# Seven products for the first group's third unit, and later stores of the direct quarters

## The chip, the cores and the metric

The kernel runs on one core of a Trainium2 chip. The core has five engines that run side by side and meet at semaphores: TensorE (PE, matrix products; its weight loads are listed as PEld), VectorE (DVE), ScalarE (ACT), GpSimd (POOL) and SyncE (SP). In this kernel GpSimd and SyncE mainly issue transfers between the chip's DRAM and the on-chip memory (SBUF), and products land in the eight banks of PSUM. Each engine executes its instructions strictly in its own order: an instruction that waits holds up everything behind it on that engine. The metric is the time on the device of one execution, in microseconds (us).

## The reference

Two stages follow each other. A causal linear attention with decay runs over q, k, v of shape (4 batches, 8 heads, 768 positions, 64), in blocks with a running state per head:

```python
intra = einsum(einsum(qb, kb) * Dmask, vb)            # within the block
inter = einsum(qb * lam_pow, kv_state)                # from the blocks before
out[:, :, sl] = intra + inter
kv_state = lam_block * kv_state + einsum(kb * rev_pow, vb)
```

Its output, seen as x of 3072 tokens x 512, goes through a two-layer block in fp32, with w_in of 512 x 2048 and w_out of 2048 x 512:

```python
h = x @ w_in
g = h - tanh(h)
out = g @ w_out
```

## The kernel before, in words

**Groups and units.** The tokens are worked in six groups (g = 0 to 5) of 512: 128 positions of each of the four batches. The hidden dimension 2048 is worked in four units (u = 0 to 3) of 512. One unit of `h` is a 512 x 512 product; its four corners, 11, 12, 21 and 22, are 256 x 256 each, and a corner sits in one PSUM bank.

**Seven products in the place of eight.** From group 1 on, a unit is made by `up` (L545): seven block products with sums of quarters as factors (a Strassen-Winograd scheme), each four matmuls of 128x128 weights by 256 columns, so 28 in the place of the 32 that the plain form takes. The sums of weight quarters are made by `sums_in(u)` (L256, four VectorE additions, the last of which overwrite a quarter of the weights), those of token quarters by `att_sums(g)` (L509, four more). A product's result is not a corner: product 1's bank `y` is copied by ScalarE into a second bank `w` (L568), on which product 2 then accumulates; products 6 and 7 go on in `y`, products 5 and 3 in `z`, and VectorE adds the parts together. From group 2 on, some of these products are themselves made of seven smaller ones ("twice": `inner_steps`, L674, and `down_twice`, L895).

**Group 0** uses the plain form for all four units (`up_plain`, L954), since the weights arrive while it runs. They come as 64-bit words (the float64 input) that must be rounded to fp32: three ScalarE operations (L291 to L293) and two VectorE operations (L295, L296) for each block of 128 x 512 (`round_block`, called through `weights`). The list `turns` (L1062) writes out in which order units 1 to 3 are computed, how many blocks are rounded after each, and which piece of the next group's attention (`p0`, `p1`) is put behind it. Then `down_first` (L985) makes group 0's second layer in eight steps kt, with seven accumulating banks; `sums_out(kt)` makes the sums of w_out's quarters, and `sums_late`, `sums_first` those of the hidden values.

**Factors in DRAM.** `sums_out` stores the seven factors of w_out to a DRAM tensor `factors`. For products that are made twice, each factor is again needed as seven quarters and sums of quarters; these lie in the DRAM tensor `fine`, one slot of 256 KB for each. Of the seven, three are plain quarters of one factor ("direct"), and four are sums. Before, the direct ones are written in `sums_out` (L276 to L279), straight from the tiles there: 24 DMA issues over the eight steps, in rows of 512 bytes. The sums are made later in `factors_twice(t)` (L772), for t = 0 to 4, from four quarters that `load_quarters(t)` (L759) has read back from `factors`: t = 0 and 1 in group 1, t = 2 at the end of group 1, t = 3 and 4 in group 2. For t = 2 to 4 the four sums are written over the loaded quarters, in the tile `gS` (the hidden tensor "S1", free just then).

**The queue of loads.** During the groups, GpSimd issues every load of a weight piece (`piece`, L785) into a ring of eight tiles `wb`: it issues a load once the product that used the ring's oldest tile is done. Its other DMAs (stores of results, of `fine`, loads of quarters) stand in the same order, and each of its DMAs also waits for the eighth one before it.

**Who sets the order.** A tile framework orders each engine's instructions by priority and dependency, save those marked with `tied` or `keep_in_program_order`, which stay in program order on their engine. It adds every semaphore wait, those for a transfer that still reads a buffer about to be overwritten among them.

Of the kernel before, what the change touches and what calls it, by code (L numbers as in the profile page):

```python
# [16 lines left out]
AL = mybir.AluOpType  # L17
# [7 lines left out]
def kernel(  # L25
# [223 lines left out]
    def pair_tiles(kt):  # L249

        if kt % 3 == 2:
            return tuple(ws[u].rearrange("p x k c -> p (x k) c")[:, 0:4] for u in (3, 2))
        wt = wst.tile([128, 8, 256], F32, name="wt", tag="w")
        return wt[:, 0:4], wt[:, 4:8]

# [7 lines left out]
    def sums_out(kt):  # L263
        bt, tt = pair[kt]
        b11, b12, b21, b22 = (bt[:, x] for x in range(4))
        t1, t2, t4, t3 = (tt[:, x] for x in range(4))
        nc.vector.tensor_tensor(t1, b12, b11, op=AL.subtract)
        nc.vector.tensor_tensor(t2, b22, t1, op=AL.subtract)
        nc.vector.tensor_tensor(t3, b22, b12, op=AL.subtract)
        nc.vector.tensor_tensor(t4, b21, t2, op=AL.subtract)  # L270
        f = factors[:].rearrange("x p k c -> p x k c")
        nc.gpsimd.dma_start(out=f[:, 0:1, kt, :], in_=bt[:, 0:1, :])
        nc.gpsimd.dma_start(out=f[:, 1:3, kt, :], in_=bt[:, 2:4, :])
        nc.gpsimd.dma_start(out=f[:, 3:NX, kt, :], in_=tt[:, 0:4, :])

        for x, j in ((1, 0),) if kt % 2 == 0 else ((2, 0), (3, 1)):  # L276
            dst = fine[:, SUB.index(x), :, kt // 2, :].rearrange("n p c -> p n c")
            nc.gpsimd.dma_start(out=dst[:, 0:1], in_=bt[:, 3:4, ts(j, 128)])
            nc.gpsimd.dma_start(out=dst[:, 1:5], in_=tt[:, 0:4, ts(j, 128)])  # L279

    def round_block(w, raw64, first):

# [129 lines left out]
    def att_state(g, bs):  # L412
        pair_ = slice(bs[0], bs[0] + 2)
        if g == 0:
            kv = bank("kv", "att", 4).rearrange("d (b p e) -> d b p e", b=2, p=NP)
            for n, b in enumerate(bs):
                kd, vn = raw[g, b]["k"], raw[g, b]["v"]
                for p in range(NP):
                    for j in range(2):
                        tc.keep_in_program_order(nc.tensor.matmul(  # L420
                            out=kv[ts(j, 64), n, p, :], lhsT=kd[:, 2 * p + j, :], rhs=vn[:, 2 * p + j, :],
                            start=n == 0 and p == 0, stop=True, skip_group_check=True))
            tc.keep_in_program_order(nc.scalar.activation(states(1)[0][:, pair_], kv, AF.Copy))
            return


        old, mid, new = (x[:, pair_] for x in states(g))
        subs = (0, 1) if g < NG - 1 else (0,)
        kv = [bank("kv", "att", 4).rearrange("d (b p e) -> d b p e", b=2, p=NP) for _ in subs]
        for p in range(NP):  # L430
            nc.scalar.activation(mid[:, :, p], old[:, :, p], AF.Copy, scale=fwd[:, p, HALF - 1:HALF])
# [77 lines left out]
    def att_sums(g, bs):  # L509
        x0, x1 = xt[g, 0], xt[g, 1]  # L510
        b11, b21, b12, b22 = x0[:, 0:2], x0[:, 2:4], x1[:, 0:2], x1[:, 2:4]
        tt = xpool.tile([128, 3, 2, HB], F32, name="tt", tag="tt")
        nc.vector.tensor_tensor(tt[:, 0], b12, b11, op=AL.subtract)
        nc.vector.tensor_tensor(tt[:, 1], b22, tt[:, 0], op=AL.subtract)
        nc.vector.tensor_tensor(b12, b22, b12, op=AL.subtract)
        nc.vector.tensor_tensor(tt[:, 2], b21, tt[:, 1], op=AL.subtract)
        xt[g] = dict(B11=b11, B21=b21, B22=b22, T1=tt[:, 0], T2=tt[:, 1], T3=b12, T4=tt[:, 2])
# [27 lines left out]
    def up(g, u, n):  # L545
# [5 lines left out]
        t, first = product_bank(key, n)  # L551
        for m in range(2):
            for kt in range(2):
                nc.tensor.matmul(out=t[:, m, :], lhsT=wt[:, kt, ts(m, 128)], rhs=x[:, kt, :],  # L554
                                 start=first and m == 0 and kt == 0, stop=kt == 1, skip_group_check=True)

        def dst(c):
            return hidden(g, c)[:, u]
# [200 lines left out]
    def load_quarters(t):  # L759

        for i in range(2):
            for j in range(2):
# [6 lines left out]
                tied(t > 1, nc.gpsimd.dma_start(out=x, in_=quarter_source(t, i, j)))  # L769
                quarters[t, i, j] = x  # L770

    def factors_twice(t):  # L772

        b11, b12, b21, b22 = (quarters.pop((t, i, j)) for i in range(2) for j in range(2))
        if t > 1:
            t1, t3, t4, t2 = b11, b12, b21, b22
        else:
            t1, t2, t3, t4 = (late["pool"].tile([128, NU, 128], F32, name=f"wt{x}", tag="sums", bufs=4)
                              for x in (1, 2, 3, 4))
        for x, dst, a, b in ((5, t1, b12, b11), (7, t3, b22, b12), (6, t2, b22, t1), (4, t4, b21, t2)):  # L780
            tc.keep_in_program_order(nc.vector.tensor_tensor(dst, a, b, op=AL.subtract))
            nc.gpsimd.dma_start(out=fine[TWICE.index(MADE[t]), SUB.index(x)], in_=dst)
            yield
# [152 lines left out]
    def every(steps):  # L936
        for _ in steps:
            pass
# [15 lines left out]
    def up_plain(u, cs):  # L954

        hm = {}
        for c in cs:
            a, t = divmod(c - 11, 10)
            tag = ("att", 4) if u == 1 else (("ya", "yb", "z", "w")[2 * t + a], 1)
            hm[c] = bank("h", *tag).rearrange("q (m c) -> q m c", m=2)  # L960
        for i in range(KI):
            for c in cs:
                a, t = divmod(c - 11, 10)
# [15 lines left out]

    def sums_first(u):  # L980
        g11, g12, g22, s1 = (hidden(0, c)[:, u] for c in (11, 12, 22, "S1"))
        nc.vector.tensor_tensor(s1, g12, g22, op=AL.add)
        nc.vector.tensor_tensor(g12, g11, g12, op=AL.subtract)

    def down_first(kt, ns):  # L985

# [65 lines left out]
    for i in range(KI - 1):  # L1052
        next(rest)
        next(rest)
        if i:
# [3 lines left out]
    every(rest)  # L1059
    sums_first(0)  # L1060
    p0, p1 = attention(1)
    turns = [(1, 11, 2, ()), (1, 21, 2, ()), (1, 12, 2, ()), (1, 22, 2, ()), (2, 11, 0, ()), (2, 21, 1, p0[0:1]),  # L1062
             (3, 11, 0, p0[1:3]), (3, 21, 1, p0[3:4]), (2, 12, 1, p0[4:]), (2, 22, 1, p1[0:1]), (3, 12, 1, p1[1:3]),
             (3, 22, 1, ())]
    for u, c, n, more in turns:
        every(up_plain(u, (c,)))
        ahead = (u, c) == (2, 12)
        if ahead:
            run(more)
        weights(ready["done"] + n, u > 1)  # L1070
        if not ahead:
            run(more)
        if c == 22:
            sums_first(u)
            if u == 1:
                ready["to"] = len(blocks)
                load(B + 2)
                load_weights(NU * KI + 2)
                load(B + 3)
                load_weights(NU * KI + WAHEAD)  # L1080
                load(2 * B)
                powers()
    sums_out(0)
    weights(NU * KI + 6, True)
    for kt in range(KH):
        down_first(kt, (1, 2))
        if kt == 0:
            run(p1[3:4])
            down_first(kt, (5,))
            run(p1[4:])  # L1090
        if kt + 1 < KH:
            sums_out(kt + 1)
        sums_late(kt)
        down_first(kt, (4, 7, 6, 3) if kt == 0 else (5, 4, 7, 6, 3) if kt + 1 < KH else (5, 6, 7, 4, 3))
        if kt + 3 < KH:
            weights(ready["done"] + 2)
        if kt in (1, 4, 6):
            sums_in((1, 4, 6).index(kt))
    first_results()
    early.close()  # L1100
    late["blk"] = ctx.enter_context(tc.tile_pool(name="blk", bufs=2 * B - 1))
# [6 lines left out]
    def make_factors(step):  # L1108
        t = TURNS.get(step)
        if t is not None:  # L1110
            if t not in making:
                making[t] = factors_twice(t)
            next(making[t])

# [4 lines left out]
    for g in range(1, NG):  # L1119
# [84 lines left out]
        if last:  # L1204
            down_end(g)
            continue
        if g < GI:
            for u in (2, 3):
                inner_weights(u, (6,))
# [5 lines left out]
        for kind, x in in_turn(g):  # L1215
# [19 lines left out]
                every(factors_twice(3))  # L1235
            if g == GI and (kind, x) == (5, 6):
                load_quarters(4)
            if g == GI and (kind, x) == (6, 7):
                every(factors_twice(4))
            if kind == 6 and x in (5, 6, 2, 7):  # L1240
# [35 lines left out]
```

## Time and profile before

| | us |
|---|---|
| runs (median of 3) | 649.3 (646.28 to 653.39) |
| the profiled execution | 649.38 |
| its span, first to last instruction | 647.6 |
| TensorE busy | 635.9 |
| VectorE / ScalarE / GpSimd busy | 477.6 / 267.3 / 228.6 |

The span is 1.8 us below the profiled execution's own time. TensorE's granted clock is full throughout. Busy times of TensorE are of pipelined instructions whose ends are modelled. "Idle before" in a row is how long the engine stood still ahead of that instruction, with what released it. A time such as 351.48 is counted from the span's start.

### The profile page before, as it was taken

How to read it: one execution, taken by the hardware profiler on the slowest of the kernel's cores; microseconds unless marked ns; L12 is line 12 of the kernel's file. 1: busy time of each engine (PE TensorE's matmuls, PEld its weight loads, DVE VectorE, ACT ScalarE, POOL GpSimd, SP SyncE). 2: the span in 40 equal slices, each digit the busy share in tenths (PEclk: the TensorE clock that was granted, in tenths of full speed). 3: DMA queues.
4: the chain of work that ended last, by engine and by line, in shares of the span. 5: the costliest groups of instructions: out<-in, count | busy, mean ns of one | idle time of the engine just before them, and what ended most of it. 6: DMA issues, size and time to landing. Idle time of an engine off the chain costs nothing.

```text
span 647.6 us, 16635 instructions
## 1 busy us (share of the span) xinstructions
PE 635.9 (98%) x6440; PEld 584.0 (90%) x6440; DVE 477.6 (74%) x948; ACT 267.3 (41%) x620; POOL 228.6 (35%) x397
## 2 busy tenths in 40 slices
PE   8899999999999999999999999999999999999998
PEld 7788888888888899998999998999998899998997
DVE  4468697785898867569967569988667987467953
ACT  4789676503432422345331247333245332334310
POOL 0000255735443454410455431355321254520161
PEclk9999999999999999999999999999999999999999
DMA  9979998969765999775889986798884577832484
GB/s 215 219 192 245 315 273 278 346 191 266 207 167 124 294 264 303 210 191 121 211 242 289 289 211 160 173 280 242 261 182 96 134 237 241 246 104 76 102 287 150
DMA packets 166190, 139.80 MB, mean 216 GB/s; under 512 B 136864, under 2 KB 138016, under 8 KB 166112
## 3 DMA queue, kind: packets, MB, share of 16 engines
q0 software_dynamic: 31792, 104.62, 51.1%
q1 hardware_dynamic: 134176, 34.12, 26.2%
q8 instruction: 51, 0.84, 0.6%
q14 instruction: 27, 0.22, 0.1%
q10 hardware_dynamic: 144, 0.00, 0.0%
HBM read 111.94 MB, written 26.74 MB: 214 GB/s over the span
## 4 chain that ended last, share of the span: by engine, by line
PE 46%; issue 19%; DMA 10%; DVE 8%; POOL 8%; SPq 6%; ACT 3%; POOLq 0%; DVEq 0%; ACTq 0%
PE acc L994 7%; PE h L965 6%; DMA q_blk<-in_q_dram 5%; PE y L906 5%; SPq L151 4%; PE plain L849 4%; PE y L554 4%; POOL wb L795 4%; PE zw L906 3%; PE y L697 3%; PE z L554 2%; POOL wb L792 2%; DMA k_blk<-in_k_dram 2%; DMA k_nat<-in_k_dram 1%; PE z L697 1%
## 5 line engine op out<-in xcount | busy, mean ns | idle before, releaser
L795 POOL DMA_DIRECT2D wb<-fine x133 | 71.7, 540 | 159.2 <-PE plain L849 108.8
L849 PE MATMUL plain<-wb,g 128*128 128x256 f32 x416 | 96.0, 381 | 0.0
L849 PEld LDWEIGHTS plain<-wb,g 128*128 128x128 f32 x416 | 77.5, 190 | 10.4
L965 PE MATMUL h<-xt,w 128*128 128x256 f32 x256 | 58.3, 382 | 1.4 <-DVE w L296 1.4
L798 POOL DMA_DIRECT2D wb<-factors x64 | 34.5, 540 | 71.2 <-PE z L697 47.9
L910 ACT ACTIVATE q<-y 128x128 f32<-128x128 f32 x76 | 21.1, 278 | 87.4 <-PE y L906 86.3
L965 PEld LDWEIGHTS h<-xt,w 128*128 128x128 f32 x256 | 47.5, 190 | 8.7 <-DVE w L296 1.8
L906 PE MATMUL y<-wb,g 128*128 128x128 f32 x336 | 44.8, 278 | 0.0
L792 POOL DMA_DIRECT2D wb<-fine_in x60 | 32.5, 544 | 28.8 <-PE z L697 10.8
L600 ACT ACTIVATE th<-g 128x512 f32<-128x512 f32 x48 | 29.4, 627 | 29.8 <-DVE g L625 29.6
L906 PEld LDWEIGHTS y<-wb,g 128*128 128x128 f32 x336 | 40.7, 192 | 0.7
L688 ACT ACTIVATE g<-y 128x512 f32<-128x512 f32 x24 | 14.3, 597 | 63.1 <-PE y L697 63.1
L404 ACT ACTIVATE k_nat<-k_nat,mask 128x64 f32<-128x64 f32 (+1 forms) x128 | 35.0, 335 | 1.7 <-DMA k_nat<-in_k_dram 1.7
L994 PE MATMUL acc<-wt,g 128*128 128x256 f32 x144 | 32.9, 380 | 0.2 <-DVE g L973 0.2
L601 DVE TENSOR_TENSOR g<-g,th 128x512 f32<-128x512 f32 x48 | 32.1, 683 | 0.4
L697 PE MATMUL z<-tt,wb 128*128 128x128 f32 x256 | 31.9, 275 | 0.0
L994 PEld LDWEIGHTS acc<-wt,g 128*128 128x128 f32 x144 | 27.2, 190 | 4.3 <-DVE g L973 0.6
L906 PE MATMUL zw<-wb,g 128*128 128x128 f32 x224 | 30.2, 278 | 0.1
L619 PE MATMUL y<-xt,w 128*128 128x256 f32 x128 | 30.3, 379 | 0.0
L619 PE MATMUL zs<-xt,ws 128*128 128x256 f32 x128 | 30.2, 379 | 0.0
L697 PEld LDWEIGHTS z<-tt,wb 128*128 128x128 f32 x256 | 30.2, 192 | 0.0
L292 ACT ACTIVATE r<-raw 128x512 int16<-128x512 uint32 x32 | 25.2, 787 | 8.8 <-DMA raw<-in_moe_w_out_dram 4.6
(236 smaller groups left out, 1475.0 us busy)
## 6 DMA issues: line engine op xcount, KB each, us to landing
wb<-fine POOLq DMA_DIRECT2D x133, 256.0 KB, 4.0
wb<-factors POOLq DMA_DIRECT2D x64, 256.0 KB, 4.3
wb<-fine_in POOLq DMA_DIRECT2D x60, 256.0 KB, 4.8
v_nat<-in_v_dram SPq DMA_DIRECT2D x24, 256.0 KB, 5.2
raw<-in_moe_w_out_dram POOLq DMA_DIRECT2D x12, 512.0 KB, 6.0
k_nat<-in_k_dram SPq DMA_DIRECT2D x20, 256.0 KB, 4.9
fine<-wt POOLq DMA_DIRECT2D x17, 256.0 KB, 3.5
raw<-in_moe_w_in_dram SPq DMA_DIRECT2D x8, 512.0 KB, 5.0
```

The source lines that it names most:

```text
L404: tc.keep_in_program_order(nc.scalar.activation(k_h, k_h, AF.Copy, scale=mask[0:rows, h % 2, h // 2, HALF - 1:HALF]))
L554: nc.tensor.matmul(out=t[:, m, :], lhsT=wt[:, kt, ts(m, 128)], rhs=x[:, kt, :], start=first and m == 0 and kt == 0, stop=kt == 1, skip_gro ...
L601: nc.vector.tensor_tensor(dst(c), src, th, op=AL.subtract)
L619: nc.tensor.matmul(out=t[:, m, :], lhsT=wt[:, kt, ts(m, 128)], rhs=x[:, kt, :], start=False, stop=kt == 1, skip_group_check=True)
L697: nc.tensor.matmul(out=dst[:, ts(u, 128)], lhsT=a, rhs=b, start=(x in (1, 5) or x == 2 and not filled) and u == 0, stop=True, skip_group_c ...
L792: nc.gpsimd.dma_start(out=t.rearrange("p m c -> p (m c)"), in_=fine_in[INNER.index(n_[1]), (5, 6, 3).index(x_)].rearrange("p u c -> p (u c)"))
L795: nc.gpsimd.dma_start(out=t.rearrange("p m c -> p (m c)"), in_=fine[TWICE.index(n_), SUB.index(x_)].rearrange("p u c -> p (u c)"))
L798: nc.gpsimd.dma_start(out=t, in_=factors[XAT[FACT[n_][1]]][:, 2 * x_:2 * x_ + 2, :])
L849: tied(held["yes"], nc.tensor.matmul(out=t[:, m, :], lhsT=a[:, u, kt, ts(m, 128)], rhs=wb[:, kt, :], start=first and u == 0 and m == 0 and ...
L906: tied(held["yes"], nc.tensor.matmul(out=dst, lhsT=a[:, u, :], rhs=wb[:, ts(u, 128)], start=x in (1, 2) and u == 0, stop=u == NU - 1, skip ...
L965: tied(u == 0 or held["yes"], nc.tensor.matmul(out=hm[c][:, m, :], lhsT=w1[u][:, i, a, ts(m, 128)], rhs=xt[0, t][:, i, :], start=m == 0 an ...
L994: tied(held["yes"], nc.tensor.matmul(out=acc[n][:, r, :], lhsT=a[:, ts(r, 128)], rhs=b, start=kt == 0 and r == 0, stop=kt == KH - 1, skip_ ...
```

## The change

1. **Direct quarters.** The 24 stores of direct quarters leave `sums_out`. A new function `quarters_alone(t)` stores the three direct quarters from the tiles of `load_quarters(t)`: 15 stores in all, in rows of 2 KB. It is called before `factors_twice(t)` for t = 0, 1, at the end of group 1 for t = 2, at the same place of group 2 for t = 3, and later in group 2 for t = 4.
2. **Unit 2 of group 0 in seven products.** `up(0, 2, n)` takes the place of four corners of `up_plain`; for it `att_sums(0)` and `sums_in(2)` run early, during unit 1. Since `ws[2]` is now in use, pairs of w_out blocks lie in `ws[1]`. Unit 3 takes its corners from the banks `w` and `yb` alone. The attention's pieces, the roundings and `powers()` (tables of decay) stand at new places of `turns`.
3. **Late sums.** `sums_first` of units 1 and 3 moves into the loop of `down_first`, tied there; the roundings of the third pair of w_out blocks come after the attention's last piece; `sums_in(2)` leaves the loop and `sums_in(1)` goes from step 4 to step 6.
4. **ScalarE's order.** In group 2 the scaling of the attention's state (L431) stays in program order.

```diff
 def pair_tiles(kt):
-            return tuple(... for u in (3, 2))
+            return tuple(... for u in (3, 1))
 def sums_out(kt):
...
-        for x, j in ((1, 0),) if kt % 2 == 0 else ((2, 0), (3, 1)):
-            dst = fine[:, SUB.index(x), :, kt // 2, :].rearrange("n p c -> p n c")
-            nc.gpsimd.dma_start(out=dst[:, 0:1], in_=bt[:, 3:4, ts(j, 128)])
-            nc.gpsimd.dma_start(out=dst[:, 1:5], in_=tt[:, 0:4, ts(j, 128)])
 def att_state(g, bs):
-            nc.scalar.activation(mid[:, :, p], old[:, :, p], ...)
+            tied(g == GI, nc.scalar.activation(mid[:, :, p], old[:, :, p], ...))
 def att_sums(g, bs):
-        nc.vector.tensor_tensor(b12, b22, b12, op=AL.subtract)
+        t3 = b12 if g > 0 else hidden(0, "S1")[:, NU - 1]
+        nc.vector.tensor_tensor(t3, b22, b12, op=AL.subtract)
 def up(g, u, n):                       # its matmuls
+                tied(held["yes"], nc.tensor.matmul(...))
+    def quarters_alone(t):
+        for x, i, j in ((1, 0, 0), (2, 1, 0), (3, 1, 1)):
+            nc.gpsimd.dma_start(out=fine[TWICE.index(MADE[t]), SUB.index(x)], in_=quarters[t, i, j])
 def up_plain(u, cs):
-            tag = ("att", 4) if u == 1 else (("ya", "yb", "z", "w")[2 * t + a], 1)
+            tag = ("w", "yb")[a] if u == NU - 1 else ("ya", "yb", "z", "w")[2 * t + a]   # u == 1: att
 def sums_first(u):                     # both operations
+        tied(u > 0, ...)
@@ the first group
-    turns = [(1, 11, 2, ()), (1, 21, 2, ()), (1, 12, 2, ()), (1, 22, 2, ()), (2, 11, 0, ()), (2, 21, 1, p0[0:1]),
-             (3, 11, 0, p0[1:3]), (3, 21, 1, p0[3:4]), (2, 12, 1, p0[4:]), (2, 22, 1, p1[0:1]), (3, 12, 1, p1[1:3]),
-             (3, 22, 1, ())]
+    for c in (11, 21, 12, 22):
+        every(up_plain(1, (c,)))
+        weights(ready["done"] + 2)
+        if c == 11:
+            att_sums(0, None)
+        if c == 21:
+            sums_in(2)
...
+    turns = [(2, 1, 0, ()), (2, 5, 0, ()), (2, 2, 0, ()), (2, 6, 0, p0[0:1]), (3, 11, 0, p0[1:3]), (2, 7, 1, ()),
+             (3, 21, 0, p0[3:4]), (2, 4, 1, p0[4:]), (3, 12, 1, p1[0:1]), (2, 3, 1, p1[1:3]), (3, 22, 1, ())]
...
+        if (u, x) == (2, 5):
+            powers()
-    weights(NU * KI + 6, True)
+    weights(NU * KI + 4, True)
     for kt in range(KH):
         down_first(kt, (1, 2))
         if kt == 0:
             ...
+            weights(NU * KI + 6, True)
...
+        if kt in (0, 3):
+            sums_first(1 if kt == 0 else NU - 1)
-        if kt in (1, 4, 6):
-            sums_in((1, 4, 6).index(kt))
+        if kt in (1, 6):
+            sums_in(kt // 6)
 def make_factors(step):
             if t not in making:
+                quarters_alone(t)
@@ groups 1 to 5, after every(p7)
+        if g in (1, GI):
+            quarters_alone(1 + g)
@@ the turn through the inner products
+            if g == GI and (kind, x) == (4, 2):
+                quarters_alone(4)
```

More of the change, by code (lines that the diff above doesn't have):

```diff
@@ L251, in pair_tiles @@
         if kt % 3 == 2:
-            return tuple(ws[u].rearrange("p x k c -> p (x k) c")[:, 0:4] for u in (3, 2))
+            return tuple(ws[u].rearrange("p x k c -> p (x k) c")[:, 0:4] for u in (3, 1))
         wt = wst.tile([128, 8, 256], F32, name="wt", tag="w")
@@ L430, in att_state @@
         for p in range(NP):
-            nc.scalar.activation(mid[:, :, p], old[:, :, p], AF.Copy, scale=fwd[:, p, HALF - 1:HALF])
+            tied(g == GI, nc.scalar.activation(mid[:, :, p], old[:, :, p], AF.Copy, scale=fwd[:, p, HALF - 1:HALF]))
         for n, b in enumerate(bs):
@@ L514, in att_sums @@
         nc.vector.tensor_tensor(tt[:, 1], b22, tt[:, 0], op=AL.subtract)
-        nc.vector.tensor_tensor(b12, b22, b12, op=AL.subtract)
+        t3 = b12 if g > 0 else hidden(0, "S1")[:, NU - 1]
+        nc.vector.tensor_tensor(t3, b22, b12, op=AL.subtract)
         nc.vector.tensor_tensor(tt[:, 2], b21, tt[:, 1], op=AL.subtract)
-        xt[g] = dict(B11=b11, B21=b21, B22=b22, T1=tt[:, 0], T2=tt[:, 1], T3=b12, T4=tt[:, 2])
+        xt[g] = dict(B11=b11, B21=b21, B22=b22, T1=tt[:, 0], T2=tt[:, 1], T3=t3, T4=tt[:, 2])
     def attention(g):
@@ L553, in up @@
             for kt in range(2):
-                nc.tensor.matmul(out=t[:, m, :], lhsT=wt[:, kt, ts(m, 128)], rhs=x[:, kt, :],
-                                 start=first and m == 0 and kt == 0, stop=kt == 1, skip_group_check=True)
+                tied(held["yes"], nc.tensor.matmul(
+                    out=t[:, m, :], lhsT=wt[:, kt, ts(m, 128)], rhs=x[:, kt, :], start=first and m == 0 and kt == 0,
+                    stop=kt == 1, skip_group_check=True))
         def dst(c):
@@ L958, in up_plain @@
             a, t = divmod(c - 11, 10)
-            tag = ("att", 4) if u == 1 else (("ya", "yb", "z", "w")[2 * t + a], 1)
-            hm[c] = bank("h", *tag).rearrange("q (m c) -> q m c", m=2)
+            tag = ("w", "yb")[a] if u == NU - 1 else ("ya", "yb", "z", "w")[2 * t + a]
+            hm[c] = bank("h", *(("att", 4) if u == 1 else (tag, 1))).rearrange("q (m c) -> q m c", m=2)
         for i in range(KI):
@@ L981, in sums_first @@
         g11, g12, g22, s1 = (hidden(0, c)[:, u] for c in (11, 12, 22, "S1"))
-        nc.vector.tensor_tensor(s1, g12, g22, op=AL.add)
-        nc.vector.tensor_tensor(g12, g11, g12, op=AL.subtract)
+        tied(u > 0, nc.vector.tensor_tensor(s1, g12, g22, op=AL.add))
+        tied(u > 0, nc.vector.tensor_tensor(g12, g11, g12, op=AL.subtract))
     def down_first(kt, ns):
@@ L1061 @@
     p0, p1 = attention(1)
-    turns = [(1, 11, 2, ()), (1, 21, 2, ()), (1, 12, 2, ()), (1, 22, 2, ()), (2, 11, 0, ()), (2, 21, 1, p0[0:1]),
-             (3, 11, 0, p0[1:3]), (3, 21, 1, p0[3:4]), (2, 12, 1, p0[4:]), (2, 22, 1, p1[0:1]), (3, 12, 1, p1[1:3]),
-             (3, 22, 1, ())]
-    for u, c, n, more in turns:
-        every(up_plain(u, (c,)))
-        ahead = (u, c) == (2, 12)
+    for c in (11, 21, 12, 22):
[5 more added lines that the diff above has]
+            sums_in(2)
+    ready["to"] = len(blocks)
+    load(B + 2)
+    load_weights(NU * KI + 2)
+    load(B + 3)
+    load_weights(NU * KI + WAHEAD)
+    load(2 * B)
+    turns = [(2, 1, 0, ()), (2, 5, 0, ()), (2, 2, 0, ()), (2, 6, 0, p0[0:1]), (3, 11, 0, p0[1:3]), (2, 7, 1, ()),
+             (3, 21, 0, p0[3:4]), (2, 4, 1, p0[4:]), (3, 12, 1, p1[0:1]), (2, 3, 1, p1[1:3]), (3, 22, 1, ())]
+    for u, x, n, more in turns:
+        if u == 2:
+            up(0, u, x)
+        else:
+            every(up_plain(u, (x,)))
+        ahead = (u, x) == (2, 4)
         if ahead:
             run(more)
-        weights(ready["done"] + n, u > 1)
+        weights(ready["done"] + n, True)
         if not ahead:
             run(more)
[L1073 to L1082, printed above, removed]
+        if (u, x) == (2, 5):
+            powers()
     sums_out(0)
-    weights(NU * KI + 6, True)
+    weights(NU * KI + 4, True)
     for kt in range(KH):
@@ L1094 @@
         down_first(kt, (4, 7, 6, 3) if kt == 0 else (5, 4, 7, 6, 3) if kt + 1 < KH else (5, 6, 7, 4, 3))
+        if kt in (0, 3):
+            sums_first(1 if kt == 0 else NU - 1)
         if kt + 3 < KH:
-            weights(ready["done"] + 2)
-        if kt in (1, 4, 6):
-            sums_in((1, 4, 6).index(kt))
+            weights(ready["done"] + 2, kt == 0)
+        if kt in (1, 6):
+            sums_in(kt // 6)
     first_results()
```

## The prediction

> **What bounds the kernel now.** The page's first part comes first, then the waits, then TensorE's rows by time. TensorE is busy for nearly the whole span:
>
> ```profile
> PE 635.9 (98%) x6440; PEld 584.0 (90%) x6440; DVE 477.6 (74%) x948; ACT 267.3 (41%) x620; POOL 228.6 (35%) x397
> ```
>
> The span is 647.6, so TensorE idles 11.7 us, about half of it before 45 us, while the first weights arrive. The change can win only by fewer matmuls or by an end of the few waits; it loses where TensorE must wait for something new. The rest is therefore read at the places where TensorE's neighbours have no slack. First, the first group (columns of a windows row: window, its length, then busy time and instructions of PE, PEld, DVE, ACT, POOL, then clock, DMA share, GB/s):
>
> ```profile
> 42.30:60.00 17.70, 17.70 (x82) 15.60 (x83) 14.73 (x31) 17.69 (x32) 0.00 (x0) 1.00 1.02 221
> ```
>
> ScalarE is busy 17.69 of 17.70 us: whatever is put on it here comes late by as much as lies ahead of it. Then TensorE's rows of the first group in which it waited (start, busy, row; idle before in brackets):
>
> ```profile
> 93.76 1.13 PE L994 MATMUL acc<-wt,g 128*128 128x256 f32 x4 [0.18 <-DVE g L973]
> ...
> 97.93 1.16 PE L501 MATMUL op<-ss,v_nat 64*64 64x64 f32 x64 [0.88 <-ACT seen L486]
> ```
>
> Then group 2, where the quarters for t = 3 are made (VectorE, then TensorE):
>
> ```profile
> 345.47 0.69 DVE L781 TENSOR_TENSOR gS<-gS 128x512 f32<-128x512 f32 x1 [1.34 <-DMA gS<-factors]
> ...
> 347.49 0.69 DVE L781 TENSOR_TENSOR gS<-gS 128x512 f32<-128x512 f32 x1 [1.12 <-DMA gS<-factors]
> ...
> 348.30 0.68 DVE L781 TENSOR_TENSOR gS<-gS 128x512 f32<-128x512 f32 x1
> 348.90 0.68 DVE L864 TENSOR_TENSOR q<-q,plain 128x512 f32<-128x512 f32 x1
> 349.50 0.68 DVE L866 TENSOR_TENSOR q<-q,plain 128x512 f32<-128x512 f32 x1
> ```
>
> ```profile
> 351.48 1.06 PE L697 MATMUL w<-xt,w 128*128 128x128 f32 x8
> 352.37 1.89 PE L849 MATMUL plain<-wb,g 128*128 128x256 f32 x8
> ```
>
> VectorE already stands still for the loads of the quarters, and TensorE's step at 351.48 follows 1.3 us after L866 has ended (350.18): the least cover in this stretch.
>
> **Part 2, fewer matmuls.** Unit 2 takes 28 in the place of 32 matmuls of 128x256. The chain of waits prices such a product:
>
> ```profile
> 156.43 1.73 PE z L554 x8
> ```
>
> These are four matmuls with their weight loads, so 1.73 / 4 = 0.4325 each: −4 × 0.4325 = **−1.73**. Bounds: 0 where the time returns as waits (below), −1.73 at most.
>
> The seven products bring three new meetings with ScalarE or VectorE.
>
> (a) Product 1's bank `y` is copied to `w` on ScalarE (L568) before product 2. The copy stands behind the three roundings of a block of unit 3's weights:
>
> ```profile
> 55.09 0.70 ACT L291 ACTIVATE w<-raw 128x512 f32<-128x512 f32 x1
> 55.66 0.80 ACT L292 ACTIVATE r<-raw 128x512 int16<-128x512 uint32 x1
> 56.29 0.79 ACT L293 ACTIVATE r<-raw 128x512 f16<-128x512 f32 x1
> 56.91 0.60 ACT L972 ACTIVATE th<-h 128x512 f32<-128x512 f32 x1
> ```
>
> They end at 56.91, where the next row starts; the copy, a 128x512 operation of 0.6, ends at 57.5. Unit 1 ends at 53.2, products 1 and 5 take 1.75 each, so TensorE wants product 2 at 56.7. Wait **+0.85** (0 if ScalarE runs one block less by then; +2.1 if it runs a block, 1.87, later).
>
> (b) Corner (3,11) needs bank `w` empty, so VectorE's g for corner 11 (L563). That waits for its tanh, which stands behind the masks (1.67 at 59.21) and a block of roundings; VectorE then has one more rounding and two copies ahead. I get g at 62.65 and TensorE ready at 61.9: **+0.75** (0 to 1.5).
>
> (c) In the second half of the attention one product (1.73) lies between the transposes and `sp`, where a corner lay (3.54 from 82.56 to 86.10). Four copies qt/kt on ScalarE, at 0.475 apart (83.33 to 84.75), now follow a block of roundings and end at about 86.65, against TensorE at 86.3: **+0.4** (0 to 1.3).
>
> `att_sums(0)` and `sums_in(2)` are eight VectorE operations of about 0.6 during unit 1. VectorE has idle time there (before 37 us and 0.8 ahead of each rounding at 50.70 and 54.80), and only a rounding (53.00) is late by one and a half microseconds, still ahead of ScalarE's need. Cost 0; uncovered they would be part of (a).
>
> **Part 3, the order.** `seen` waits behind a block of roundings and four state scalings (95.28 to 97.73), and TensorE waits 0.88 for it, and 0.18 for g. In the new order `seen` follows one rounding directly and the corner's g lies earlier: **−1.06** (0 to −1.06). The late sums stand in the loop with 34.4 of 45 us of VectorE busy between 99 and 144; the narrowest is `sums_late(1)` at 105.1 against a use at 105.5: 0, bound +1.
>
> **Part 1, the stores.** 24 issues leave GpSimd between 69 and 138; raw loads go out earlier, but what they feed is gated by ScalarE: 0 (0 to −0.5). The 15 new stores are 3.75 MB that `sums_out` wrote before.
>
> For t = 0 and 1 they stand between loads at 153 to 160 whose data are used near 189; for t = 2 the stores land near 248 and VectorE's sums stand at 257.50; for t = 4 they land near 378 and the sums stand at 381. Each 0. For t = 2, 0.75 MB at 293 GB/s is 2.6 us of transfers in a window whose DMA share is 0.98:
>
> ```profile
> 232.00:262.00 30.00, 30.00 (x316) 27.81 (x315) 21.47 (x57) 7.62 (x19) 16.86 (x29) 1.00 0.98 293
> ```
>
> The ring is asked 10 to 12 us ahead and its loads land in 4.3 to 8.3: 0, bound +1.
>
> For **t = 3** no such slack is there. The sums overwrite the quarters, so each must wait for the store that reads its destination. GpSimd's order is: issue the store of quarter 11, which waits for the first load (344.6); one ring load; quarter 21's store, which waits for the third load (346.4); quarter 22's, which waits for the fourth. That one landed at 347.45, as the wait of 1.12 above shows. VectorE: the first sum waits for the first store, the third one (`t2`, at 348.30 before) for the last store. The price of a store from issue to landing, from the DMA issues (KB each, median):
>
> ```profile
> gS<-factors POOLq DMA_DIRECT2D x4, 256.0 KB, 7.8
> ...
> fine<-gS POOLq DMA_DIRECT2D x2, 256.0 KB, 3.7
> ```
>
> I take 3.7, the same store in the same window (346 to 350); the tile's own range over the run is 3.0 to 8.1. GpSimd issues that store about 0.1 after the fourth load, at 347.6, so `t2` starts at 347.6 + 3.7 = 351.3, three microseconds late, and L864 and L866 behind it. They read the bank `z` of product 7, which TensorE's step at 351.48 waits for. L866 ends 1.95 after `t2` starts, at 353.25: wait **+1.8** (+1.1 at 3.0; 6.1 at 8.1; nothing if the store lands by 349.5). The next meeting, a bank freed at 355.95 for the step at 357.62, moves by 3.0 against TensorE's 1.8 and still holds by half a microsecond. Ring loads behind the stores go out 4 to 6 us later and land before use.
>
> By the Trainium skill ("DMA: Bandwidth & Descriptors", section "Anatomy of one DMA — SWDGE (gpsimd) path") a transfer costs a fixed 2.0 us plus its bytes over 436 GB/s, an estimate of 2.6 us for 256 KB, which would make the wait about 0.7 and the sum −0.1. The rows, 3.0 to 8.1, lie above it, and the measurement decides.
>
> **Part 4** keeps four scalings of 0.3 each in order at 201 and 226; VectorE needs them at 206 and 227.1: 0, bound +0.5.
>
> **Sum.** −1.73 − 1.06 + 0.85 + 0.75 + 0.4 + 1.8 = +1.0. The profiled execution took 649.38 and the median is 649.3, so the same base: **650.4**.
>
> **Rivals.**
>
> *Nothing is late.* The copies of (a) to (c) find ScalarE early and the store lands in 3.0: −1.73 − 1.06 + 1.1 = −1.7, so **647.7**; 646.5 with every wait gone. For it: each early wait is under 0.9, the size of my error in following ScalarE's order. Against it: ScalarE's 17.69 of 17.70. Chance 0.27.
>
> *VectorE is held for the store's landing* (the slower side). In group 2 the last of the three stores lands in 8.1, the longest row, not 3.7, because the ring's loads, issued just before and after, share the 16 DMA engines with it (their mean share is 0.98 from 336 to 362). `t2` starts at 355.6, TensorE waits 353.25 + 4.35 − 351.48 = 6.1; sum +5.3: **654.7** (653 to 657.5 with (a) to (c) at their upper ends). It decides from a landing of 349.5 on, and each microsecond beyond costs one. For it: the loads of the same tile took 7.8 at the median. Against it: both stores of the window took 3.0 to 4.8. Chance 0.16.
>
> *The stores in `sums_out` were in the way.* If the 24 issues in rows of 512 bytes held up w_out's blocks, their going would win where `acc` waits; but the waits show only the 0.18 above there. About −3, so 646.5 or less. Chance 0.04.
>
> **How the numbers follow.** My forecast (649 to 652.5) has 0.53. The range 646 to 655.5 reaches over the first rival and most of the second; outside are the far ends of the second and third. One per cent, 6.5 us, is about what a measurement of this kernel can tell from no change (its three runs lie 7 apart). Faster by it needs 642.8: only the far end of the third rival, 0.03. Slower needs 655.9: nearly half of the second rival, 0.07. Same 0.90.
>
> **What would show it.** In the new profile: 28 L554-kind and L965-kind matmuls for unit 2; the waits for `seen` and g near 94 to 98 gone; idle before product 2 from ScalarE's `w`, before (3,11) from VectorE's g, before `sp` from kt, each under 1; near 347 to 353 VectorE idle before its quarter sums from DMA `fine<-gS`, GpSimd idle from DMA `gS<-factors`, and TensorE idle 1.8 before the step after L866. I am wrong if TensorE's idle total does not grow by about 2.7 (the sum's +1.0 plus 1.73), or if VectorE's sums show no wait for a store.

## The result

| | before | after | ratio (95% interval) |
|---|---|---|---|
| median of 20 runs each, us | 647.51 | 650.74 | 1.0040 (1.0024 to 1.0057) |
| the same once more, 23 and 12 runs | 647.36 | 648.94 | 1.0027 (1.0013 to 1.0040) |
| profiled execution (span) | 649.38 (647.6) | 651.84 (650.1) | |

By these ratios the changed kernel is slower by 0.3 to 0.4%, 1.7 to 2.6 us, which is within the one per cent called "same". A ratio here is not the quotient of the two medians, which lie 3.2 and 1.6 us apart; sizes against before are taken from the ratios. The forecast was 650.4, +1.0 us on a base of 649.4. The time fits better than the change does: the median of the three runs of before that were shown, and its profiled execution, lay 1.8 and 1.9 us above the median of twenty. Both profiled executions lie above their medians (by 1.9 and 1.1), so a difference of the two traces is good for the place of a wait, not for the last microsecond of the sum.

The page's first part for the kernel after:

```profile
PE 636.0 (98%) x6432; PEld 582.2 (90%) x6432; DVE 481.0 (74%) x954; ACT 269.5 (41%) x623; POOL 221.2 (34%) x388
```

TensorE has 8 records less, the four matmuls, each with two records; its idle time is 650.1 − 636.0 = 14.1 us in place of 11.7. Its waits by size (columns: who waited for what; us in total, times, longest):

```profile
PE z L550 <- DVE g L577: 1.9, 1, 1.9
PE kv L432 <- issue: 1.5, 1, 1.5
...
PE w L550 <- ACT w L565: 0.8, 1, 0.8
...
PE h L966 <- DVE g L560: 0.7, 1, 0.7
...
PE w L694 <- DVE q L867: 0.3, 1, 0.3
PE sp L357 <- ACT kt L337: 0.3, 1, 0.3
```

Apart from the gap put down to issue, the five shown are new. Four are those that the prediction worked out; the largest, on L577, is not among them. Where the time went is seen when the start of the same matmul is compared in both traces:

| place in before, us | after minus before, us | what happened since the line above |
|---|---|---|
| 28.3 | −1.1 | before waited 1.1 for a load of v and 0.7 for weights; in after the load was there |
| 99.0 | −1.4 | the first group: −0.3 |
| 173.5 | +0.7 | 1.87 of waiting for L577's g: +2.2 |
| 304.3 | +1.9 | a 1.5 us gap put down to issue; before had 0.6 and 0.35 of such gaps |
| 351.5 | +1.9 | 0.31 behind L867; lesser shifts back before it |
| 540.1 | +3.5 | gaps put down to issue, 0.29 and 0.41, with restarts |
| 621.8 | +2.5 | before waited 0.87 for a load here, after did not |

The gaps put down to issue stand inside bursts of 64x64 matmuls and come and go: the twelve traces of this study have between 0 and 2.2 us of them, the two of the changed kernel itself 2.2 and 0.6. So they are not put down to the change. What is, is the first group, the wait at 173.5 and the one at 351.5.

**The wait that was not foreseen.** VectorE in the kernel after (start, busy, row; idle before in brackets):

```profile
164.42 0.69 DVE L572 TENSOR_TENSOR g<-g,z 128x512 f32<-128x512 f32 x1
170.51 0.69 DVE L782 TENSOR_TENSOR wt<-wq 128x512 f32<-128x512 f32 x1 [5.40 <-DMA fine_in<-ws]
...
173.52 0.68 DVE L577 TENSOR_TENSOR g<-g,z 128x512 f32<-128x512 f32 x1
```

The sum for t = 0 writes into one of four buffers that it shares with `inner_weights`, so it waits until a store to `fine_in` has read that buffer. Now it waits 5.40 and starts at 170.51, and L577, whose bank TensorE needs, stands behind it. In the kernel before:

```profile
168.47 0.69 DVE L781 TENSOR_TENSOR wt<-wq 128x512 f32<-128x512 f32 x1 [2.05 <-DMA fine_in<-ws]
```

The stores were issued at the same time (from 164.2 before, 164.1 after), but the three took 6.0 us at the median to land, against 4.0 before. There was little room for that: in the kernel before, L577's counterpart ended at 172.17, 1.3 us before TensorE used it at 173.53. In the kernel after, VectorE is 2.0 later and TensorE, 1.1 ahead of before by what it gained earlier, would have come at 172.4; so it waits 1.87. GpSimd's rows in the kernel after say what had been put in front of the stores:

```profile
153.72 0.56 POOL L771 DMA_DIRECT2D fine<-wq  x1 [1.65 <-DMA wq<-factors]
...
157.50 0.54 POOL L771 DMA_DIRECT2D fine<-oq  x1 [1.36 <-DMA oq<-factors]
158.56 0.54 POOL L771 DMA_DIRECT2D fine<-oq  x1 [0.52 <-DMA oq<-factors]
159.09 2.13 POOL L799 DMA_DIRECT2D wb<-factors  x4
```

In the kernel before, the ring's loads begin at:

```profile
152.85 1.09 POOL L798 DMA_DIRECT2D wb<-factors  x2
```

Five of the six stores of direct quarters wait on GpSimd, one by one, and the four loads of the ring stand behind them: they go out at 159.1 to 161.2, where before they went at 152.9 to 156.2. The last direct store landed at 162.4, but the four loads land 5.6 to 7.1 after their issue, the last of them near 167.8, so they are still under way when the stores to `fine_in` follow at 164.1.

**The wait of group 2.** VectorE in the kernel after:

```profile
349.25 0.69 DVE L782 TENSOR_TENSOR gS<-gS 128x512 f32<-128x512 f32 x1 [3.66 <-DMA fine<-gS]
...
351.37 0.69 DVE L782 TENSOR_TENSOR gS<-gS 128x512 f32<-128x512 f32 x1 [0.43 <-DMA fine<-gS]
351.98 0.68 DVE L865 TENSOR_TENSOR q<-q,plain 128x512 f32<-128x512 f32 x1
352.58 0.68 DVE L867 TENSOR_TENSOR q<-q,plain 128x512 f32<-128x512 f32 x1
```

The sum `t2` starts at 351.37 (forecast 351.3) and L867 ends at 353.26 (forecast 353.25). TensorE came to its step at 353.10, 1.6 us later than in before, and waited 0.31 and not 1.8:

```profile
353.41 1.13 PE L694 MATMUL w<-xt,w 128*128 128x128 f32 x8 [0.31 <-DVE q L867]
```

The agreement of the two times is luck. The loads of the quarters went out 1.3 us later too, before and after:

```profile
337.05 2.98 POOL L769 DMA_DIRECT2D gS<-factors  x4
338.31 2.98 POOL L766 DMA_DIRECT2D gS<-factors  x4
```

They stand on GpSimd behind ring loads that wait for TensorE's products, so TensorE's lateness moves them along. Counted from the start of these loads, `t2` was forecast at 14.25 (351.3 − 337.05) and came at 13.06: the last of the three stores went out about 1.0 sooner and took about 0.2 less than forecast. From the same start TensorE came at 14.79 in place of 14.43. Together that is the 1.5 by which the wait is shorter.

### The profile page after: what moved, and what is told of

It reads as the page before. It is cut to its first block, busy times and chain, and to the rows that moved or that the text cites. A ratio compares the mean times of both kernels' runs of the same rounds, so it can differ in the third digit from the quotient of the medians.

```text
span 650.1 us, 16608 instructions
## 1 busy us (share of the span) xinstructions
PE 636.0 (98%) x6432; PEld 582.2 (90%) x6432; DVE 481.0 (74%) x954; ACT 269.5 (41%) x623; POOL 221.2 (34%) x388
## 4 chain that ended last, share of the span: by engine, by line
PE 60%; DMA 16%; SPq 10%; DVE 6%; ACT 5%; issue 3%; POOL 0%; ACTq 0%; DVEq 0%; POOLq 0%
SPq L151 9%; PE y L907 8%; PE plain L850 8%; PE y L694 8%; DMA q_blk<-in_q_dram 7%; PE zw L907 6%; DMA k_blk<-in_k_dram 5%; PE z L694 4%; PE h L966 4%; PE y L616 3%; PE zs L616 3%; PE y L550 2%; PE w L694 2%; PE op L496 1%; DMA k_nat<-in_k_dram 1%
## 5 line engine op out<-in xcount | busy, mean ns | idle before, releaser
L966 PE MATMUL h<-xt,w 128*128 128x256 f32 x192 | 44.0, 383 | 1.5 <-DVE w L291 0.7
L966 PEld LDWEIGHTS h<-xt,w 128*128 128x128 f32 x192 | 35.6, 190 | 7.4 <-DVE w L291 1.2
L216 POOL DMA_DIRECT2D raw<-in_moe_w_out_dram x12 | 6.7, 562 | 88.7 <-DMA v_nat<-in_v_dram 73.2
```

The lines of the kernel that those rows point to most:

```text
L966: tied(u == 0 or held["yes"], nc.tensor.matmul(out=hm[c][:, m, :], lhsT=w1[u][:, i, a, ts(m, 128)], rhs=xt[0, t][:, i, :], start=m == 0 an ...
```

## The experiments

Theory A: the loss not foreseen is the wait at 174, made by the order on GpSimd. Rival B: the loss lies in the first group's seven products. Rival C: the wait at 174 is luck of the transfers. The kernel before was run beside each set; its median was 647.25, 648.80 and 647.36 in the three sets, so ratios are compared.

### Part 1 undone (stores_back)

```diff
@@ the changed kernel, sums_out
+        for x, j in ((1, 0),) if kt % 2 == 0 else ((2, 0), (3, 1)):
+            ...                                  # the two stores, as before
@@
-                quarters_alone(t)                # and its two other calls
```

> The changed kernel without part 1: the 24 stores of direct quarters are back in sums_out, the 15 later ones are gone; parts 2 to 4 stay. Theory A (the loss that was not foreseen is the wait of 1.87 us at 174, which comes from the six later stores of t = 0 and 1 standing ahead of the ring's loads and of the stores to fine_in): no wait of TensorE for L577's g near 174, VectorE's sums of quarters in group 2 wait for loads alone, and the first group keeps its waits for w, g and kt of 0.8, 0.7 and 0.3; against before -1.73 - 1.06 + 0.84 + 0.70 + 0.28 = -1.0 us. Rival B (the loss lies in the seven products of the first group): about +2.6, as the whole change. Rival C (the wait at 174 is luck of the transfers): a wait of 1 to 2 us near 174 here too.

Measured: 652.54, ratio 1.0082 (1.0064 to 1.0100): +5.3 us, slower than the whole change. Near 174 TensorE does not wait, the first group's waits are 0.9, 0.6 and 0.3, and VectorE's sum for t = 0 waits 1.95 as in before. But two other losses stand in the trace. VectorE:

```profile
123.92 0.43 DVE L295 TENSOR_SCALAR wt<-wt 128x512 uint32<-128x512 uint32 x1 [3.30 <-DMA fine<-wt]
```

TensorE, at the first of them and then in group 2:

```profile
126.57 1.13 PE L996 MATMUL acc<-wt,g 128*128 128x256 f32 x4 [2.10 <-DVE g L1004]
...
296.61 1.99 PE L621 MATMUL y<-xt,w 128*128 128x256 f32 x8 [1.10 <-ACT y L611]
```

With the 24 stores back, a rounding of w_out must wait for the store of a direct quarter that still reads its tile, and TensorE waits 2.1 for what stands behind. Near 300 TensorE waits three times, 1.10 as shown, then 0.68 and 1.10 for `zs`. These go back to ScalarE waiting 5.66 for `k_nat`, whose load SyncE issued at 291.7 (284.7 in before); SyncE's small loads, which run one after another from 130 on, were slower from the first set on (12.56 us for 16 in place of 9.74) and again near 235 (17.83 in place of 11.32). What slowed them, the second time above all, is not shown, and masks_pool below has some of these waits too (0.3 and 1.1 for zs). So the expected −1.0 is wrong and so is B's account: parts 2 to 4 alone lose 5 us, but not by their own products, whose waits are nearly those of the whole change. The wait at 126 is one place where their new order needs part 1.

### Part 1 alone (stores_only)

```diff
@@ the kernel before, sums_out
-        for x, j in ...                          # the 24 stores
@@
+    def quarters_alone(t): ...                   # and its three calls
```

> The kernel before with part 1 alone. Theory A: the wait near 174 is there, about 2 us, and in group 2 TensorE's step after L867's sum waits longer than in the changed kernel, 1 to 1.8 us, since it is not late itself; together +3 to +4 us. Rival B: 0 to +1 us. Rival C: a wait near 174 of any size between 0 and 2.

Measured: 649.66, ratio 1.0037 (1.0024 to 1.0050), +2.4 us. The wait for L577's counterpart is there, 1.49 at 174.5, and after it 0.17; the wait in group 2 is 0.2. That is less than the +3 to +4 expected, and the listed waits make 1.8 of the 2.4. Part 1 alone has the loss of the whole change, and B falls: with part 1 in place, parts 2 to 4 together add little either way (1.0040 and 1.0027 against 1.0037). The size in group 2 was expected too high, and not because TensorE was late: it came to the step at 351.34, where it came at 351.48 in before. `t2` started at 349.46 and not at 351.3.

### The six stores twice (double_direct)

```diff
             if t not in making:
+                quarters_alone(t)
                 quarters_alone(t)
```

> The changed kernel with the stores of t = 0 and 1 issued twice each, six more transfers of 256 KB at the same place. Theory A: the stores to fine_in land later still, and VectorE's wait for them and with it TensorE's near 174 grows from 1.9 to 3.5 to 6 us: +2 to +4 against the changed kernel. Rivals B and C: the wait stays below 2.5 and the time within 1 us of the changed kernel.

Measured: 655.42, ratio 1.0122 (1.0105 to 1.0139). TensorE:

```profile
178.03 3.78 PE L550 MATMUL z<-tt,ws 128*128 128x256 f32 x8 [5.14 <-DVE g L577]
```

GpSimd:

```profile
158.99 1.23 POOL L771 DMA_DIRECT2D fine<-wq  x2 [3.03 <-DMA fine<-wq]
...
168.98 0.76 POOL L650 DMA_DIRECT2D fine_in<-ws  x1
```

The wait is 5.14, within the forecast of 3.5 to 6, but partly in another way than forecast. The second store of a quarter writes the same slot of `fine`, and GpSimd stands still for the first one to land (3.03, later 1.57). So the stores to `fine_in` are issued at 169.0 and later in place of 164.1, and land 3.3 to 5.0 us after it, not later than in the changed kernel. The run shows that what stands ahead on GpSimd moves TensorE's wait, and C falls for the cause; it doesn't separate the bytes from GpSimd's standing still. In group 2 the wait is 1.5. What the 3.78 shows is told in the last section.

### The six stores behind the sums (late_direct)

```diff
             next(making[t])
+            if step in (10, 17):
+                quarters_alone(t)                # kept in order behind fine_in's stores
```

> The changed kernel with the six stores of t = 0 and 1 moved on GpSimd behind the sums of the same quarters (those of t = 0 to where VectorE's fourth sum is done, those of t = 1 likewise one unit later); nothing else moves on any engine. Theory A: the ring's loads go out near 152 to 156 as before, the stores to fine_in land in about 4 us in place of 6, the wait of 1.87 near 174 is gone and nothing takes its place: 1.9 us faster than the changed kernel, +0.7 against before. Rival B: as the changed kernel. Rival C: a wait of 0 to 2 near 174 that has nothing to do with the order.

Measured: 649.90, ratio 1.0043 (1.0030 to 1.0057): nothing won. The wait at 174 is gone, and one unit later stands its like:

```profile
185.70 1.99 PE L550 MATMUL z<-tt,ws 128*128 128x256 f32 x8 [1.12 <-DVE g L577]
188.10 1.99 PE L550 MATMUL y<-xt,w 128*128 128x256 f32 x8 [0.41 <-ACT g L569]
```

GpSimd now waits 3.43 for the direct stores of t = 0 to land before it may load into their buffers, and the next unit's stores to `fine_in` follow at 177 right behind three ring loads; VectorE waits 4.64 for them. The mechanism is A's; "nothing takes its place" was wrong.

### The ring's loads first (ring_first)

```diff
+    def send(n):
+        while sent["n"] < min(n, len(stream)):   # the loop taken out of piece()
     load_quarters(1)
+    send(4)
     up(1, 0, 1)
```

> The changed kernel with the first four loads of the ring put ahead of the six stores of t = 0 and 1 on GpSimd, so that they fill the time in which GpSimd stands still for the quarters' landing; nothing else moves. Theory A2 (the wait at 174 comes from the ring's loads being pushed in front of the stores to fine_in, and in late_direct it only went one unit on, to 185, because there the direct stores themselves stood in front of the next stores to fine_in): with both out of the way no wait of TensorE for L577's g at 174 nor at 185; 2 us faster than the changed kernel, +0.6 against before. Rival D (the 1.5 MB more that must be written in this stretch cost their time wherever they stand): a wait of 1 to 2 us again, at one of the two places or near 189, and +2 to +3 against before.

Measured: 650.02, ratio 1.0012 (0.9987 to 1.0037). No wait at 174 nor at 185. GpSimd's rows:

```profile
153.14 0.54 POOL L797 DMA_DIRECT2D wb<-factors  x1 [0.51 <-DMA wq<-factors]
...
155.16 0.55 POOL L771 DMA_DIRECT2D fine<-wq  x1 [0.58 <-DMA oq<-factors]
```

The same transfers, in another order: between 148 and 176 the DMA engines are busy 0.95 and move 280 GB/s, 0.89 and 255 in the kernel after. VectorE's wait falls from 5.40 to 2.92, and the stores to `fine_in`, issued at 164.1 as in the changed kernel, land in 3.7 at the median. All traces agree on this. Where the six stores stand ahead of the ring's loads (after, after_again, stores_only) that landing took 6.0, 5.0 and 5.5; in ring_first and in the four runs below that keep its order it took 3.5 to 3.8, and TensorE does not wait there in any of them. So Rival D (the bytes cost their time anywhere) falls by the traces; the time alone, +0.8 with an interval that reaches from −0.8 to +2.4, can't separate it. In group 2 TensorE now waits 0.84: `t2` starts 13.6 after the quarters' loads, in place of 13.06.

### Masks on GpSimd (masks_pool)

```diff
@@ on top of ring_first, powers()
-                tc.keep_in_program_order(nc.scalar.activation(mask[...], whole[j][...], AF.Copy))
+                nc.gpsimd.tensor_copy(mask[...], whole[j][...])
```

> ring_first, and the four mask copies of powers() (1.67 us of ScalarE) made by GpSimd, which is idle there. If the wait for g before corner (3,11) is ScalarE's, as the prediction had it, ScalarE's tanh of corner 11 comes 1.3 to 1.7 us earlier and TensorE's wait of 0.70 there is gone; the wait of 0.84 before product 2 stays, since the copy stands ahead of the masks: 0.7 to 0.9 us faster than ring_first, about 0 against before. If it is VectorE's, the wait stays.

Measured: 649.48, ratio 0.9992 (0.9967 to 1.0017). TensorE does not wait for g before corner (3,11) any more, and the wait before product 2 stays (0.86). So the former was ScalarE's, as forecast. The 0.7 us is within the intervals of the two runs; the trace shows it, the times alone don't.

### The copy ahead of the roundings (copy_first)

```diff
@@ on top of masks_pool
-        weights(ready["done"] + 2)
+        weights(ready["done"] + (2 if c != 22 else 0))
-    turns = [(2, 1, 0, ()), ...
+    turns = [(2, 1, 2, ()), ...                  # and the copy of L565 stays in order
```

> masks_pool with product 1's copy y to w ahead of the roundings of the third block of unit 3's weights on ScalarE; nothing else moves. If ScalarE's amount of work sets the place of these waits, the 0.84 before product 2 is gone and comes back, 0.5 to 0.9, before corner (3,11), since all four blocks must be rounded before the tanh: within 0.4 us of masks_pool. If only the order set it, both waits are gone and it is 0.9 us faster.

Measured: 647.86, ratio 0.9968 (0.9947 to 0.9988). ScalarE:

```profile
53.94 0.62 ACT L975 ACTIVATE th<-h 128x512 f32<-128x512 f32 x1
54.41 0.63 ACT L564 ACTIVATE w<-y 128x512 f32<-128x512 f32 x1
54.92 0.71 ACT L285 ACTIVATE w<-raw 128x512 f32<-128x512 f32 x1
```

Both waits are gone (0.05 is left before the corner). I expected the wait to come back there, because I held that ScalarE would have to stand still for product 1; it did not, the bank was ready at 54.4. With the masks away ScalarE has slack, and the order alone set this wait. The trace shows it; the intervals of this run and of masks_pool overlap.

### The sums of t = 3 later (sums_later)

```diff
@@ on top of masks_pool
-            if g == GI and (kind, x) == (1, 5):
+            if g == GI and (kind, x) == (1, 2):
                 every(factors_twice(3))
```

> masks_pool with VectorE's four sums of quarters for t = 3 behind the two additions that read product 7's bank, two steps later. The wait of TensorE in group 2 after those additions (0.31 in the changed kernel, 1.5 in double_direct), which grows when TensorE comes there earlier, is gone and VectorE does not wait for stores of quarters: 0.3 to 1 us faster than masks_pool, -0.5 against before. Rival: the sums' own stores or VectorE's later work come late for a ring load, and a wait of TensorE for wb shows between 355 and 400.

Measured: 648.32, ratio 0.9990 (0.9966 to 1.0015). VectorE makes the two additions at 344.65 and 345.25, the sums from 351.86 on, and waits for no store; TensorE waits neither behind the additions nor for a load between 355 and 400. The gain over masks_pool in time lies within the intervals.

### All of it, and the change once more (all_four, after_again)

all_four is copy_first with sums_later's edit.

> copy_first and sums_later together: the ring's loads first, the masks on GpSimd, product 1's copy ahead of the roundings, the sums for t = 3 two steps later. By the waits that each took away (1.87 + 0.17 near 174, 0.84 before product 2, 0.70 before corner (3,11), 0.3 to 1.0 after product 7's additions) and the 0.1 to 0.2 us that TensorE loses beside each: 4 to 4.5 us faster than the changed kernel, -1.5 to -2.5 us against before (ratio 0.996 to 0.998). Rival: the earlier TensorE meets the next wait (SyncE's late k_nat near 290, a ring load), and it stands at copy_first's 0.997 or above.

Measured: 645.74 against 647.36, ratio 0.9980 (0.9964 to 0.9997), −1.3 us, and 0.5% faster than the changed kernel of the same set (648.94). That is less than forecast (−1.5 to −2.5, and 4 to 4.5 us under the changed kernel, where it is 3.2), and it stands where the rival put it, no lower than copy_first's 0.997; that it is faster than copy_first is not shown, though neither of the waits that the rival named is in the trace. Of TensorE's new waits kt's 0.3 is left, and 0.75 at 22.9, at a place where before waited 1.11 for a load. It beats both kernels, a little.

> The changed kernel once more, beside all_four on one chip. Theory A: the wait of TensorE for L577's g near 174 is there again, 1.5 to 2 us, and the three waits of the first group are again 0.8, 0.7 and 0.3, since they come from orders; the gaps put down to issue near 227, 305, 442 and 543 differ from the first profile, since they come and go. Ratio to before 1.003 to 1.005. Rival C: the wait near 174 is missing or under 1 us.

Measured: ratio 1.0027 (1.0013 to 1.0040). The three waits of the first group are 0.8, 0.7 and 0.3 again. The ratio is just under the 1.003 forecast. The wait near 174 is there, but 0.73, under the 1.5 to 2 forecast and under the 1 us that was named for rival C: VectorE's sum started at 169.77 after 4.26 of waiting, against 170.51 and 5.40. That there is a wait comes from the order, as ring_first and its followers show; its size in one execution depends on when the transfers land, and so much of rival C is right. In group 2 TensorE does not wait here; the issue gaps are 0.6.

## Why the prediction was right, and where it was not

- **Four matmuls, −1.73; waits for `seen` and g, −1.06.** There are 8 records less, and neither wait is in the list. But TensorE's busy time doesn't fall by 1.73: over the first group (28.29 to 103.44 before, 27.16 to 101.90 after, between the same matmuls) it is 73.83 and 72.55, 1.28 less, and over the whole span 635.9 and 636.0.
- **(a), (b), (c): 0.85, 0.75, 0.4.** Measured 0.84, 0.70, 0.28, and masks_pool and copy_first showed the causes named: ScalarE's masks for (b), and its roundings ahead of the copy for (a). Yet the first group gained 0.3 to 0.4 and not 0.8. The idle time grew by 0.87, near the 0.76 of the measured waits (0.84 + 0.70 + 0.28 − 1.06); what is missing is the 0.45 of busy time above. A group of matmuls behind a wait, or behind a burst of small ones, is listed longer (1.99 for eight records in place of 1.89); such restarts were no term of the sum. That they make up the whole 0.45 is argued, not shown.
- **Part 1, t = 0 and 1: "Each 0".** This is the step that failed. It looked at who reads the stored data (near 189) and not at what is queued behind the stores: the ring's loads and, behind those, the stores to `fine_in`, for which VectorE already waited 2.05 in before, with 1.3 us left to TensorE's use. Measured: 0.73 to 1.87 of waiting, some 1 to 2.2 us with restarts. The step asked of every moved DMA what it holds up on its own queue for t = 3, where no slack was expected, and not here.
- **t = 3, +1.8.** The mechanism was right: the sums wait for the direct stores, and TensorE for L867. The size was off (0.31, and 0 in the second trace). The sum took the loads' landing and TensorE's step as fixed times of before's trace, but both follow TensorE, since the loads are issued behind its products. In all eight traces with these stores and the sums in their old place, TensorE reaches the step 14.8 us after the loads begin, however late it is. So the wait is set by how soon `t2` comes: 12.7 to 13.1 after the loads in five traces (waits of 0 to 0.31), 13.6 and 13.7 in ring_first and copy_first (0.84, 0.95), 14.25 in double_direct (1.50). The forecast had 14.25 as well. Why the transfers take longer in three of them is not shown. The store forecast at 3.7 took about 3.5 (347.8 to 351.4). The Trainium skill's estimate of 2.6 for such a transfer ("DMA: Bandwidth & Descriptors", section "Anatomy of one DMA — SWDGE (gpsimd) path") is too low here.
- **The base.** Three runs gave 649.3; twenty gave 647.5. With that base and the sum of +1.0 the forecast would have been 648.5.
- **The rivals.** "Nothing is late" did not happen; "VectorE held for 8.1" did not: that store landed in 3.5, and the 8.1 was a load's, since the stores of that tile in before took 3.0 to 4.7 between 346 and 353. "The stores in `sums_out` were in the way" had more to it than its 0.04: not in the kernel before, but in the new order, as the wait of 2.10 in stores_back shows.

The range held the time and "same" was the class; +1.0 was a mis-sized sum whose two errors (t = 0 and 1 too low, t = 3 too high) went against each other. The sign that was named, an idle total that grows by about 2.7, came out at 2.4, and that was luck too: the waits that had been worked out make 1.1 of it (0.84 + 0.70 + 0.28 + 0.31 − 1.06), and the one at 174 makes 1.87.

## What to carry to other kernels

When transfers are moved, follow the queue and not the data: ask what is issued behind them, which engine waits for those, and how long it waits already; a wait of 2 us that ends just in time is the first to become the bound. Here it paid to issue the loads that needn't wait ahead of the stores that must. When a forecast time comes out, ask whether the engine that it is compared with has moved along. And two parts of a change can need each other: part 1 alone loses, parts 2 to 4 alone lose more, and the order that covers both wins a little.

## What the runs showed of the hardware

The wait of 5.14 us in double_direct cost more than itself. Windows of that kernel (window, its length, busy time and instructions of PE, PEld, DVE, ACT, POOL, clock, DMA share, GB/s):

```profile
174.00:175.00 1.00, 0.00 (x0) 0.00 (x0) 0.00 (x0) 0.00 (x0) 0.48 (x1) 1.00 0.94 299
175.00:176.00 1.00, 0.00 (x0) 0.00 (x0) 0.63 (x1) 0.00 (x0) 0.00 (x0) 0.58 0.94 322
...
178.00:182.00 4.00, 3.97 (x9) 3.16 (x10) 3.23 (x6) 2.55 (x7) 1.75 (x4) 0.50 0.80 221
182.00:184.00 2.00, 2.00 (x11) 1.75 (x10) 1.93 (x9) 0.28 (x1) 1.30 (x2) 1.00 1.06 349
```

TensorE's last matmul before the wait ended at 172.9. The granted clock was still 1.00 up to 175 and fell in the next microsecond (0.58 is its mean there), so about 2.3 us after TensorE had stopped. It was 0.50 for the first four microseconds of work after the wait, and eight records took 3.78 in place of 1.89; from 182 on it was 1.00 again. That is about 2 us on top of the wait. After the waits of 1.87 (after) and 2.10 (stores_back) the matmuls took 1.99 and 1.13, as at full clock.

The Trainium skill ("TensorE: Matmul & The Clock Gate", section "Part 1: The HAM clock gate") says that the clock falls to half after an idle window of some 3.4 us and rises again after as long a time of work. The trace agrees with the fall to half and, roughly, with the time of work (4.0), but here the clock fell sooner, after 2.3 us of standing still; this is one execution.
